# Attention feeding a gated feed-forward layer: visits of the attention stages one unit later, transposes of q behind the spread of the reciprocals, and finer dependencies of the output weights

## The chip, the core and the metric

The kernel runs on one core of one Trainium2 chip. The metric is the device time of one execution in microseconds (us); lower is better. Three runs of the kernel before gave a median of 535.46 us (535.23 to 538.49).

The core has a matrix engine (PE), a vector engine (DVE), an activation engine (ACT) and two engines that here do hardly more than start transfers: SP for stores, transposes and small copies, POOL for loads. Each engine works through its own instructions strictly in the order in which they stand in its program, and waits where one of them depends on something that isn't done.

## The reference

```python
def _attn_ref(q, k, v, E, F):            # q, k, v: 8 batches, 8 heads, 1024 x 64
    k_proj = np.einsum('ks,bhsd->bhkd', E, k)     # 1024 rows become 64
    v_proj = np.einsum('ks,bhsd->bhkd', F, v)
    scores = scale * np.matmul(q, k_proj.transpose(0, 1, 3, 2))
    ...
    attn = np.exp(scores)
    attn = attn / (np.sum(attn, axis=-1, keepdims=True) + 1e-09)
    return np.matmul(attn, v_proj)

def _moe_ref(x, w_gate, w_val, w_out):   # x: 8192 x 512, weights 512 x 1536 and 1536 x 512
    gate = 1.0 / (1.0 + np.exp(-(x @ w_gate)))
    val = x @ w_val
    return gate * val @ w_out
```

The attention's output, with its eight heads side by side, is `x` of the second function. All arrays are float32; the kernel computes in bfloat16 on PE with float32 sums.

## The kernel before, in words

**Blocks and units.** The 8192 rows are 16 blocks of 512, two for each batch. The feed-forward layer of a block is cut into three *units* K = 3 * block + (0, 1, 2); a batch b is units 6b to 6b+5, called u = 0 to 5. In one unit `g_chain` (L1746) computes a sixth of the gate and `v_chain` (L1775) a sixth of the value columns, each with seven half-size products of 4 matmuls (a Strassen-like scheme, so it needs sums of blocks of `x` and of weights beforehand: `xs_sums` L1589, `gt_sums` L1548, `vt_sums` L1519, all on DVE). Once a block's three units are done, `o_chain` (L1428) multiplies by the output weights `wO` with seven products in 14 groups of 6 matmuls, with the weight sums of `t_sums` (L1316): T2, T3 and T4 go to the tile `wT`, and T1 replaces the quarter B12 inside `wO`. Stores of the finished rows (`stored`, L1413) leave on SP.

**Attention.** While the feed-forward units of batch b run, the attention of batch b+1 is computed in short *visits* that borrow four of the eight PSUM banks (A0, F0, A3, F3, of which A0 and F0 are those of `g_chain`): `sc_visit` (L1170) computes the scores of four heads, and ACT takes their exponentials; there are two such visits. `den_visit` (L1186) follows the second: the denominators on PE, two reciprocals on DVE (`rec`, L959), and `spread` (L1126), which writes the reciprocals to DRAM (tile `rden` to `rd`, on SP) and, when that has landed, reads them back with eight broadcasting transfers of 256 KB (`xu<-rd` in the profile, L1146). `xo_visit` (L1178), twice, multiplies by v; `scaled` (L1155) on DVE multiplies the result with the spread reciprocals into `xT`, the input of the next batch's units. The first `xo_visit` needs the first four of the eight transfers. Then `kv` (L863) projects k and v of batch b+2 into 64 rows on PE; `keep_kd` (L879) copies the k part on ACT to `kpd`, and one transposing transfer on SP makes `kpD` of it, which the next `sc_visit` needs. `transpose_q` (L850) makes `qT` of the loaded `Qb` with four transposing transfers on SP. `load_q`, `load_k`, `load_v` (L423, L395, L405) bring 1 MB each from POOL. There is one `Qb`, one `qT`, one `kpD` and one pair of buffers for k and v.

**The places of the visits.** They are set in the loop over b, `late_` being 1 for b = 1 and 0 otherwise:

```python
            late_ = 1 if b == 1 else 0
...
                    if u == late_:
                        n["sc_visit"](t0 - 1.0, (0, 1), (GA, GC, XA, XB))
                    if u == late_ + 1:
                        n["sc_visit"](t0 - 1.0, (2, 3), (GA, GC, XA, XB))
                        n["den_visit"](t0 + 6.0, XA)
                        if b + 2 < B:
                            transpose_q()
```

So the visits of b = 1 lie in units 1, 2, 4, 5 (with `kv` in 5), and those of b = 2 to 6 in units 0, 1, 3, 4 (with `kv` in 4).

**What sets the order.** From unit 6 on, everything is noted as tasks, and `arranged` (L52) puts them in order: it goes through a model of the engines with fixed costs (`COST`, L28) and takes, whenever an engine is free, the ready task with the earliest due time. Due times come from the goals that are given to groups of matmuls (`PACE` is 9.9 us for a unit). The resulting order, not its times, becomes the program; `Plan.add` (L146) then finds what each instruction has to wait for, from the names that it reads (`r`) and writes (`w`). Units 0 to 5 are put in order by hand (`todo`, `put`, `on`, L1876 to L1977); their last steps are `kv2` (L1962), two of the weight sums (T4 and T1, `on(3, 4, ...)`, L1971) and the transposes of q (L1972). The first task of the planned part, `o_chain(1, ...)` (L1992), uses bank A2, which `kv2` used just before.

Of the kernel before, what the change touches and what calls it, by code (L numbers as in the profile page):

```python
# [7 lines left out]
ALU = mybir.AluOpType  # L8
# [22 lines left out]
class Task:  # L31
    def __init__(self, eng, call, t):
        self.eng, self.calls, self.goal = eng, [] if call is None else [call], None
        busy, tail = COST[eng]
        self.busy = busy if t is None else t
        self.lat = self.busy + tail
        self.dma = call is not None and call[5] is not None
        if self.dma:
            self.busy, self.lat = (0.85 if eng == "POOL" else 0.6), t if t is not None else 3.0
# [2 lines left out]
        return later.pre[self.n]  # L42

    def keys(self):
        r, w = set(), set()
        for c in self.calls:
            r.update(c[2])
            w.update(c[3] + c[4])
        return r - w, w, (r & w)
# [66 lines left out]
class Plan:  # L116
# [8 lines left out]
        self.tasks = None  # L125
        self.open = None

    def note(self, eng, call, t):
        if self.open is not None:
            assert eng == "PE"  # L130
            self.open.calls.append(call)
        else:
            self.tasks.append(Task(eng, call, t))

    @contextlib.contextmanager
    def group(self, goal, us):
# [6 lines left out]
        self.tasks.append(self.open)  # L143
        self.open = None

    def add(self, eng, fn, r=(), w=(), x=(), dma=None, t=None):  # L146
        if self.tasks is not None:
            self.note(eng, (eng, fn, tuple(r), tuple(w), tuple(x), dma), t)
            return None
        op = Op()  # L150
        op.eng, op.fn, op.dma, op.need = eng, fn, dma, False
        op.sem, op.val = None, 0
        deps = {}

        def dep(o, raw):
            if o is op:
                return
            if o.eng == eng and o.dma is None:
                if eng == "PE" or (eng != "POOL" and not raw):
                    return  # L160
            deps[id(o)] = o

        for k in r:
            for o in self.writers.get(k, ()):
                dep(o, True)
        for k in tuple(w) + tuple(x):
            for o in self.writers.get(k, ()):
                dep(o, False)
            for o in self.readers.get(k, ()):
                dep(o, False)  # L170
        for k in r:
            self.readers.setdefault(k, []).append(op)
        for k in tuple(w) + tuple(x):
            self.writers[k] = [op]
            self.readers[k] = []
        op.deps = list(deps.values())
        for o in op.deps:
            o.need = True
        if dma is not None:
            self.dma_count[dma] = self.dma_count.get(dma, 0) + 16  # L180
            op.sem, op.val = dma, self.dma_count[dma]
        self.ops.append(op)
        return op
# [46 lines left out]
def bass_linformer_attn__then__ffn_glu_sigmoid_kernel(  # L230
# [18 lines left out]
    with contextlib.ExitStack() as es:  # L249
# [6 lines left out]
        wT = sbuf("wT", [P, 3, NF // 2, 256], BF16)  # L256
# [54 lines left out]
        wO = sbuf("wO", [P, NF, DM], BF16)  # L311
        sigs = [sbuf(f"sig{i}", [P, 2, 512], FP32) for i in range(3)]
        sig = [sigs[i][:, 0, :] for i in range(3)]
        hT = [sbuf(f"hT{i}", [P, NF, 512], BF16) for i in range(2)]
# [17 lines left out]
        add = plan.add  # L332
# [514 lines left out]

            return qt, sc, den, bc, xo

        def transpose_q():  # L850
            for r in range(NR):
                add(
                    "SP",
                    lambda e, r=r: e.dma_start_transpose(
                        qT[:, 2 * r : 2 * r + 2, :].rearrange("p h (t c) -> p (h t) c", c=P),
                        Qb[:, 2 * r : 2 * r + 2, :].rearrange("p h c -> p (h c)"),
                    ),
                    r=[("Q", hf, r // 2) for hf in range(2)],
                    w=[("qT", r)] + [("qT", hf, r // 2, r % 2) for hf in range(2)],
                    dma=f"qT{r}",  # L860
                )

        def kv(b, bk):  # L863
# [413 lines left out]
        def oproj(blk, tt, pb, cols=((0, DM),)):  # L1277
            o = vsnap[tt][:, :] if tt < 2 else ost[:, tt, :]
            ok = [("vsnap", tt)] if tt < 2 else None
            t = 2 * (2 * (blk % 2) + tt % 2) + tt // 2  # L1280
            for n, (c0, c1) in enumerate(cols):
                if n:
                    pb = FF.take()
                for m in range(NF):
                    mm(
                        pb,
                        bank[pb][:, 0 : c1 - c0],
                        hT[blk % 2][:, m, tt * P : (tt + 1) * P],
                        wO[:, m, c0:c1],
                        [("hT", blk % 2, m, tt // 2), "wO"],  # L1290
                        start=(m == 0),
                        stop=(m == NF - 1),
                    )
                dve(
                    lambda e, pb=pb, c0=c0, c1=c1: e.tensor_scalar(
                        o[:, c0:c1], bank[pb][:, 0 : c1 - c0], 0.5, None, op0=ALU.mult
                    ),
                    [],
                    ok or [("ost", tt, x) for x in ((0, 1) if len(cols) == 1 else (n,))],
                    b=pb,  # L1300
                )
                FF.append(pb)
                add(
                    "SP",
                    lambda e, c0=c0, c1=c1: e.dma_start(out_v[blk // 2, t][:, c0:c1], o[:, c0:c1]),
                    r=ok or [("ost", tt, x) for x in ((0, 1) if len(cols) == 1 else (n,))],
                    dma=f"out{tt}" if n == 0 else "outlast",
                )
# [7 lines left out]
        def t_sums(n):  # L1316
            B11, B12 = wO[:, 0:H6, 0:256], wO[:, 0:H6, 256:512]
            B21, B22 = wO[:, H6:NF, 0:256], wO[:, H6:NF, 256:512]
            T4, T3, T2 = [wT[:, i, :, :] for i in range(3)]
            o, a, b, op, r, w = {  # L1320
                3: (T3, B22, B12, ALU.subtract, ["wO"], [("wT", 3)]),
                2: (T2, T3, B11, ALU.add, ["wO", ("wT", 3)], [("wT", 2)]),
                4: (T4, B21, T2, ALU.subtract, ["wO", ("wT", 2)], [("wT", 4)]),
                1: (B12, B12, B11, ALU.subtract, [], ["wO", ("wT", 1)]),
            }[n]
            if n == 4:
                w = w + ["bsel8", ("kp", 0), ("kp", 1)]
                w += [(k, R) for k in ("rhi", "rhl") for R in range(2)]
            dve(lambda e: e.tensor_tensor(o, a, b, op), r, w, t=0.95)
# [532 lines left out]
        def second_loads():  # L1862
            load_q(1)
            load_k(1)
            load_v(1)
            transpose_q()
            load(
                wO[:, :, :],
                moe_w_out.rearrange("(m p) c -> p m c", p=P),
                ["wO"],  # L1870
                "wO",
                r=turned()[:2],
            )
# [54 lines left out]
        def on(u, j, fn):  # L1928
            put(11 + 9 * u + j, fn)
# [38 lines left out]
            AA.append(bk)  # L1968

        on(3, 4, kv2)  # L1970
        on(3, 4, lambda: (t_sums(4), t_sums(1)))  # L1971
        on(3, 4, transpose_q)  # L1972
        for i, slot in enumerate(todo):
            slot()
# [14 lines left out]
        gt_sums(1)  # L1989
        for n in (1, 2, 3, 4):  # L1990
            xs_sums(2, n)
        o_chain(1, OA, OC, 0.0, 2.0, sums=False)  # L1992
        for n in (1, 2, 3, 4):
            xs_sums(3, n)
# [2 lines left out]
        for b in range(1, B):  # L1997
            n = attention(b + 1) if b + 1 < B else None
            if b + 2 < B:
                load_k(b + 2)  # L2000
                load_v(b + 2)
            late_ = 1 if b == 1 else 0
            for u in range(6):
                K = 6 * b + u
                t0 = when(K)
                if n is not None:
# [3 lines that stand above are left out]
                        n["sc_visit"](t0 - 1.0, (2, 3), (GA, GC, XA, XB))  # L2010
                        n["den_visit"](t0 + 6.0, XA)
                        if b + 2 < B:
                            transpose_q()
                        if b + 3 < B:
                            load_q(b + 3, n["spread_keys"])
                    if u == late_ + 3:
                        n["xo_visit"](t0 - 1.0, (0, 1), (GA, GC, XA, XB))
                    if u == late_ + 4:
                        n["xo_visit"](t0 - 1.0, (2, 3), (GA, GC, XA, XB))
                        for i in (1, 2, 3, 4):  # L2020
                            xs_sums(2 * b + 2, i)
                    if u == late_ + 4 and b + 2 < B:
                        with group(t0 + 5.0, 1.83):
                            kv(b + 2, XA)
                        keep_kd(XA)
                        vd_one(XA, 0)
                        vd_one(XA, 1)
# [46 lines left out]
```

## Time and profile before

| what | us |
|---|---|
| median of three runs | 535.46 (535.23 to 538.49) |
| the profiled execution: its whole time | 538.83 |
| its span, first to last instruction | 537.0 |
| PE busy in the span | 508.6 (95%) |
| DVE busy | 405.2 (75%) |
| ACT busy | 352.0 (66%) |
| mean granted clock of PE | 0.983 |

The profile is of one execution. A row of a timeline has the start in us, the duration, the engine (SPq is a transfer started by SP), the line of the kernel, the operation, the tiles as out<-in, the shapes, and how many instructions in a row were merged; in brackets stands how long the engine was idle before it, and what ended that. Nearly all matmuls have line L372, the helper `mm`, so one goes by tiles: `pA<-qT,kpD` are scores, `pA<-eT,dsel` denominators, `pA<-eT,vpD` the products with v, `pA<-KVs,EFT` is `kv`, and `pA<-xT,wG` the first product of a unit's `g_chain`. The trace also records when each transfer has landed.

PE works without a gap of more than 0.2 us in most of the span. By the waits, it is idle four times for longer than half a microsecond after 84 us.

### The profile page before, as it was taken

Reading aid. Unit: us, or ns where it says so; the run is one execution under the profiler, and the core shown is the slowest. Engines: PE = TensorE matmul, PEld = TensorE weight load, DVE = VectorE, ACT = ScalarE, POOL = GpSimd, SP = SyncE. Lnnn points to the kernel's source line nnn. Section 1 sums busy time; section 2 is a strip of 40 time slices with the busy share of each in tenths; the row PEclk is TensorE's granted clock in tenths of the full one; section 3 lists DMA queues with packets and bytes.
Section 4 is the critical chain, followed back from the end, with each engine's and each line's share of the span. In section 5 each row is a group of like instructions: output and inputs, shape, how many; then the busy total and the mean of one; then the engine's idle time right before and its main releaser. Section 6 shows DMA issues by size and latency. Waiting matters only on the chain.

```text
span 537.0 us, 11363 instructions
## 1 busy us (share of the span) xinstructions
PE 508.6 (95%) x4668; PEld 401.6 (75%) x4677; DVE 405.2 (75%) x670; ACT 352.0 (66%) x644; POOL 36.9 (7%) x52
## 2 busy tenths in 40 slices
PE   5999998996788999999999999999999999999996
PEld 4544544884666887888788887888788888888885
DVE  3648689674675879696978879696978879786874
ACT  2555663874365856887678856887678857676752
POOL 9310200100010001000010001000000000000000
PEclk9999998999698999999999999999999999999999
DMA  9999999898969297995969395966502090101113
GB/s 162 199 199 202 149 210 176 138 188 180 139 101 188 50 193 163 149 176 98 201 98 214 56 227 83 184 141 113 134 12 79 24 222 3 51 30 40 40 41 118
DMA packets 90692, 69.42 MB, mean 129 GB/s; under 512 B 35472, under 2 KB 82832, under 8 KB 90640
## 3 DMA queue, kind: packets, MB, share of 16 engines
q0 software_dynamic: 33984, 29.89, 36.8%
q1 hardware_dynamic: 56656, 38.81, 32.9%
q8 instruction: 36, 0.59, 0.5%
q14 instruction: 16, 0.13, 0.1%
HBM read 72.88 MB, written 17.56 MB: 168 GB/s over the span
## 4 chain that ended last, share of the span: by engine, by line
PE 88%; DMA 5%; DVE 3%; ACT 1%; issue 1%; POOL 1%; SPq 0%; DVEq 0%; ACTq 0%; POOLq 0%
PE pA L372 49%; PE pF L372 39%; DMA KVs<-in_v_dram 2%; DMA kpD<-kpd 2%; DMA xu<-rd 1%; DVE vsnap L1664 1%; DVE hT L1786 0%; DVE xT L800 0%; ACT kpd L376 0%; DVE hT L1264 0%; ACT vpD L376 0%; SPq L1146 0%; DVE hS L1345 0%; POOL KVs L390 0%; POOL Qb L390 0%
## 5 line engine op out<-in xcount | busy, mean ns | idle before, releaser
L376 ACT ACTIVATE sig<-pA 128x512 f32<-128x512 f32 x126 | 74.9, 595 | 51.2 <-PE pA L372 51.2
L1653 ACT ACTIVATE pF<-pA 128x512 f32<-128x512 f32 x99 | 58.0, 587 | 43.0 <-PE pA L372 29.9
L1664 DVE TENSOR_TENSOR vsnap<-pF,vsnap 128x512 f32<-128x512 f32 x90 | 62.0, 689 | 29.4 <-ACT vsnap L376 13.9
L1740 DVE TENSOR_TENSOR sig<-pF,sig 128x512 f32<-128x512 f32 x84 | 57.5, 684 | 23.1 <-PE pF L372 17.6
L372 PE MATMUL pF<-wO,hT 128*128 128x256 bf16 (+1 forms) x400 | 59.3, 286 | 0.2 <-issue 0.2
L1786 DVE SCALAR_TENSOR_TENSOR hT<-sig,vsnap 128x512 bf16<-128x512 f32 x84 | 57.2, 686 | 1.3
L376 ACT ACTIVATE sig<-sig 128x512 f32<-128x512 f32 x84 | 52.8, 630 | 7.8 <-DVE sig L1740 7.0
L372 PE MATMUL pF<-xS,wV 128*128 128x256 bf16 x360 | 55.0, 276 | 0.3
L376 ACT ACTIVATE vsnap<-pA 128x512 f32<-128x512 f32 x84 | 50.0, 595 | 7.4 <-PE pA L372 7.2
L372 PE MATMUL pA<-xT,vT 128*128 128x256 bf16 x336 | 51.0, 275 | 0.0
L372 PE MATMUL pF<-xT,wG 128*128 128x256 bf16 (+1 forms) x257 | 49.3, 312 | 1.5 <-DVE hT L1264 0.8
L372 PE MATMUL pA<-xT,gT 128*128 128x256 bf16 x336 | 50.5, 273 | 0.0
L372 PE MATMUL pF<-xS,wG 128*128 128x256 bf16 x336 | 50.4, 273 | 0.0
L376 ACT ACTIVATE sig<-pF 128x512 f32<-128x512 f32 x66 | 39.3, 596 | 14.9 <-PE pF L372 12.9
L372 PE MATMUL pA<-wT,hT 128*128 128x256 bf16 x360 | 48.8, 273 | 0.0
L372 PEld LDWEIGHTS pF<-wO,hT 128*128 128x128 bf16 x402 | 38.6, 98 | 10.9 <-issue 1.0
L372 PEld LDWEIGHTS pF<-xS,wV 128*128 128x128 bf16 x360 | 34.4, 99 | 10.7 <-issue 2.3
L372 PE MATMUL pF<-xT,wV 128*128 128x256 bf16 (+1 forms) x240 | 41.5, 294 | 0.0
L372 PEld LDWEIGHTS pA<-xT,vT 128*128 128x128 bf16 x336 | 31.6, 98 | 9.1 <-ACT sig L376 4.1
L372 PEld LDWEIGHTS pA<-wT,hT 128*128 128x128 bf16 x360 | 35.0, 98 | 4.6 <-issue 0.4
L1786 DVE SCALAR_TENSOR_TENSOR hT<-sig,pF 128x512 bf16<-128x512 f32 x42 | 28.6, 681 | 10.8 <-PE pF L372 10.6
L372 PEld LDWEIGHTS pF<-xS,wG 128*128 128x128 bf16 x336 | 32.9, 98 | 3.8
(150 smaller groups left out, 876.1 us busy)
## 6 DMA issues: line engine op xcount, KB each, us to landing
out_dram<-ost SPq DMA_DIRECT2D x61, 256.0 KB, 3.8
xu<-rd SPq DMA_DIRECT2D x48, 256.0 KB, 7.6
Qb<-in_q_dram POOLq DMA_DIRECT2D x7, 1024.0 KB, 9.3
KVs<-in_k_dram POOLq DMA_DIRECT2D x7, 1024.0 KB, 11.2
KVs<-in_v_dram POOLq DMA_DIRECT2D x7, 1024.0 KB, 16.0
wO<-in_moe_w_out_dram POOLq DMA_DIRECT2D x1, 1536.0 KB, 13.1
wG<-in_moe_w_gate_dram POOLq DMA_DIRECT2D x5, 256.0 KB, 18.2
wV<-in_moe_w_val_dram POOLq DMA_DIRECT2D x5, 256.0 KB, 18.8
```

Source lines behind the costliest of these rows:

```text
L372: return add("PE", lambda e: e.matmul(o, lhsT, rhs, **kw), r=r, x=[("bank", b)])
L376: return add("ACT", lambda e: e.activation(o, i, func, scale=scale), r=r, w=w, x=x, t=t)
L1653: lambda e: e.activation(bank[c][:, :], bank[a][:, :], AF.Copy, scale=1.0),
L1664: lambda e: e.tensor_tensor(o, bank[bk][:, :], o, ALU.add),
L1740: dve(lambda e: e.tensor_tensor(o, bank[bk][:, :], o, ALU.add), [key], [key], b=bk)
L1786: lambda e: e.scalar_tensor_tensor(o, sg.rearrange("p (j c) -> p j c", j=2), 1.0, x.rearrange("p (j c) -> p j c", j=2), ALU.add, ALU.mult,),
```

## The change

1. `late_` is 1 for every b. The visits of b = 2 to 6 lie in units 1, 2, 4, 5 like those of b = 1, one unit later than before, with everything that hangs on them: the reciprocals and their spread, the transposes and the load of q, `kv` with the transposing transfer of `kpD`, and the sums of `x` for the next batch's first block.
2. In the planned part `transpose_q` gets the names of the spread reciprocals as a *tie*. A tie counts as something read when `arranged` makes the order, and nowhere else: the four transposes are put behind the eight spread transfers in SP's order, but no wait is added to the program.
3. The weight sums T4 and T1 leave the handwritten part and become tasks of the planned part, behind the first sums of gate weights and of `x`.
4. The quarter B12 of `wO`, which T1 overwrites, gets a name of its own, `wO12`. T1 now reads `wO` and writes `wO12`; products that read other quarters no longer wait for it, and T3 and the undivided output product (L1289) read both names.

```diff
@@ class Task @@
+        self.tie = ()
...
     def keys(self):
-        r, w = set(), set()
+        r, w = set(self.tie), set()
@@ class Plan @@
-    def note(self, eng, call, t):
+    def note(self, eng, call, t, tie):
...
             self.tasks.append(Task(eng, call, t))
+            self.tasks[-1].tie = tie
...
-    def add(self, eng, fn, r=(), w=(), x=(), dma=None, t=None):
+    def add(self, eng, fn, r=(), w=(), x=(), dma=None, t=None, tie=()):
@@ transpose_q @@
-        def transpose_q():
+        def transpose_q(tie=()):
...
                     dma=f"qT{r}",
+                    tie=tie,
@@ oproj @@
-                        [("hT", blk % 2, m, tt // 2), "wO"],
+                        [("hT", blk % 2, m, tt // 2), "wO", "wO12"],
@@ t_sums @@
-                3: (T3, B22, B12, ALU.subtract, ["wO"], [("wT", 3)]),
+                3: (T3, B22, B12, ALU.subtract, ["wO", "wO12"], [("wT", 3)]),
...
-                1: (B12, B12, B11, ALU.subtract, [], ["wO", ("wT", 1)]),
+                1: (B12, B12, B11, ALU.subtract, ["wO"], ["wO12", ("wT", 1)]),
@@ second_loads @@
-                ["wO"],
+                ["wO", "wO12"],
@@ the handwritten part @@
-        on(3, 4, lambda: (t_sums(4), t_sums(1)))
         on(3, 4, transpose_q)
@@ the planned part @@
         for n in (1, 2, 3, 4):
             xs_sums(2, n)
+        t_sums(4)
+        t_sums(1)
         o_chain(1, OA, OC, 0.0, 2.0, sums=False)
...
-            late_ = 1 if b == 1 else 0
+            late_ = 1
...
                         if b + 2 < B:
-                            transpose_q()
+                            transpose_q(n["spread_keys"])
```

More of the change, by code (lines that the diff above doesn't have):

```diff
@@ L144, in group @@
         self.open = None
-    def add(self, eng, fn, r=(), w=(), x=(), dma=None, t=None):
+    def add(self, eng, fn, r=(), w=(), x=(), dma=None, t=None, tie=()):
         if self.tasks is not None:
-            self.note(eng, (eng, fn, tuple(r), tuple(w), tuple(x), dma), t)
+            self.note(eng, (eng, fn, tuple(r), tuple(w), tuple(x), dma), t, tie)
             return None
```

## The prediction

> **What bounds the kernel now.** The page comes first: PE is busy for 95% of the span, so only PE's idle time and what it does at half clock can be won without taking work away. Its row of granted clock has three dips.
>
> ```profile
> PE 508.6 (95%) x4668; PEld 401.6 (75%) x4677; DVE 405.2 (75%) x670; ACT 352.0 (66%) x644; POOL 36.9 (7%) x52
> PEclk9999998999698999999999999999999999999999
> ```
>
> Next the waits of PE after 84 us, which name the idle time; its three long pieces lie at the three dips.
>
> ```profile
> PE pA L372 <- DVE xT L1159: 8.3, 1, 8.3
> PE pA L372 <- DMA kpD<-kpd: 4.0, 1, 4.0
> PE pA L372 <- ACT vpD L376: 2.5, 1, 2.5
> PE pA L372 <- DVE hS L1345: 0.7, 1, 0.7
> ```
>
> Then the windows (length, busy us and instructions of each engine, granted clock, DMA): what follows the shortest of the three, the other two with what follows them, and the rest.
>
> ```profile
> 88.74:92.00 3.26, 3.26 (x17) 2.28 (x18) 3.26 (x7) 0.58 (x1) 0.00 (x0) 0.52 1.01 87
> 128.95:137.21 8.26, 0.00 (x1) 0.01 (x1) 0.75 (x2) 0.28 (x1) 0.00 (x0) 0.73 0.96 186
> 137.21:143.10 5.89, 5.89 (x28) 4.09 (x29) 3.53 (x6) 2.33 (x4) 0.43 (x1) 0.51 0.90 131
> 159.64:163.62 3.98, 0.00 (x0) 0.00 (x0) 0.23 (x1) 1.25 (x3) 0.00 (x0) 0.99 1.33 158
> 163.62:167.27 3.65, 3.65 (x22) 2.14 (x23) 0.72 (x2) 2.17 (x4) 0.00 (x0) 0.55 1.18 258
> 170.00:525.00 355.00, 354.73 (x3321) 297.86 (x3318) 290.19 (x456) 255.56 (x468) 7.87 (x9) 1.00 0.54 109
> ```
>
> After each wait PE runs at about half clock (0.52, 0.51, 0.55) for three to six us; from 170 to 525 us it is busy for 354.73 of 355 us. What is saved before 170 us therefore reaches the end, if the change opens no new gap later. Last, SP's timeline before the first wait:
>
> ```profile
> 120.58 1.23 SPq L854 DMA_TRANSPOSE qT<-Qb  x1
> 121.86 0.58 SPq L1129 DMA_DIRECT2D rd<-rden  x1
> 122.54 2.62 SPq L854 DMA_TRANSPOSE qT<-Qb  x2
> 125.20 1.07 SPq L1418 DMA_DIRECT2D out_dram<-ost  x2
> 126.32 6.07 SPq L1146 DMA_DIRECT2D xu<-rd  x8
> ```
>
> The reciprocals are done at 118.15 (DVE's row 116.38, 1.77 us). But SP's next instruction is a transpose that waits for q, landed at 120.57; `rd` leaves at 121.86 and lands at 123.90, and two more transposes and two stores stand ahead of the spread. Its fourth transfer, the last that the first `scaled` needs, lands at 136.24; DVE starts at 136.46, and PE, whose next product needs that bank, at 137.21.
>
> **The change, part by part.** A unit is one of the groups K; batch b is the round of the loop.
>
> *Transposes behind the spread, batch 1* (already at units 1, 2, 4, 5). `rd` can leave at 118.2. It lands after 2.0 us (this row) or 2.4 us (244.35 to 246.79, batch 3), here beside the end of the load of q; I take 120.6. The two stores are ready once DVE's row 119.21 (0.68) is over, so they take 119.9 to 121.0 by their 1.07 us, and the spread starts at 121.0. From its start to its fourth landing: 9.9 us here (126.32 to 136.24), 9.4 in batches 2 and 3 (246.81 to 256.21); behind stores, 9.9. So 130.9, plus the 0.97 us from landing to PE: 131.9. PE would wait 2.95 instead of 8.26 us: **5.3 saved**. Bounds: 0 (something else holds `rd`), and 8.26 (a spread that lands by 128.0).
>
> *The half clock behind it.* The 28 matmuls from 137.21 take 5.89 us; at 0.109 us each (the step in the full-clock rows) they take 3.06: 2.83 lost. After the wait of 3.99 us, 8 score matmuls (0.56 us in the row at 99.60) and 14 others (1.53) took 3.65: 1.56 lost. After the wait of 2.46 us, 16 took 3.24 instead of 1.75: 1.49 lost. For a wait of 2.95, between the last two, I take 1.5: **1.3 saved** (bounds 0 and 2.83).
> [...]
>
> *Scores of batch 2 one unit later.* Before, `kv` of batch 1 (151.72, unit 5) is followed by a visit in unit 0, and the transposing transfer lands at 163.58 where PE wants it at 159.64. The visit goes to unit 1, about ten us later. The wait of 3.99 goes, and its half clock, 1.56: **5.55 saved**. In later batches, where `kv` and scores are as far apart as they will be here, the visit starts 14.9 us after `kv` (211.23 to 226.09) and the transfer has landed 12.2 to 13.0 us after it (batch 4: 332.10, 345.14). Late next is that transfer, with about two us to spare.
>
> *Visits of batches 2 to 6 one unit later.* The same instructions in another place: 0 in PE work. What changes is what lies beside them.
> (a) Spread against the first `xo_visit`. In batch 3 the fourth transfer lands at 256.21, `scaled` starts at 256.43 and ends at 257.12, and PE's next `g_chain` starts at 257.73: so a landing until 256.8 (257.73 less 0.23 and 0.69) costs nothing: 0.6 us to spare, and the limit is 15.1 us after the denominators' start (241.66). In unit 2 the store pair that starts at 255.34, 27.8 us behind the batch's first product (227.53), comes at nearly the moment of `rd` (244.35 plus a unit of 10.1, 26.9 behind). Behind `rd`, it costs the spread 0.5 us (9.9 against 9.4); ahead of it, its 0.85 us of issue and the landing behind 512 KB (2.3 and 2.7 us for the pair of 125.20). Also one group of output products less falls between denominators and `xo_visit`, 0.66 us, since the goals of two chains leave a hole there. Against this stand batches 4 and 6, which land 1.5 and 2.0 us before they must. Bounds for a batch: 0 and 2 us of wait; nearest is batch 1's row, stores between `rd` and spread: 0.3. Five batches: **1.5 lost** (0 to 10, and half clock on top if waits reach 2.46 us). No gain is possible, as PE has no gaps there.
> (b) The four transposes (1.3 us of issue each; 2.8 and 4.3 us in batch 2, where two stand behind the spread) now always come behind it. Behind them wait on SP the next stores, due a half unit or more earlier or a unit later, and `kpD`, 20 us later. On POOL the load of q waits for the transposes: in batch 2 the last two land 16.3 us after the spread's start (186.65, 202.96); in batch 3 the load of q begins 15.4 after it (262.23). With all four behind the spread I estimate 19, or 24 after the denominators' start; the load takes 8.8 us (262.23) and ends at 33, where the loads of k and v begin (32.4: 241.66 to 274.09), beside which `kpD` travels. That can take its two us to spare, and is costed at 0 (0 to 1.5 for each of four batches).
> (c) `x` for the next batch is needed one unit sooner. Batch 1 shows that place: second `xo_visit` at 148.44, its sums done at 156.4, next first product at 159.6 or later had PE not waited. 0; without that cover, up to 3 us a batch.
>
> *T4 and T1 into the plan.* Two instructions of 0.95 us leave DVE's rows 86.53 and 87.39 and are placed later among its tasks. PE's start at 88.74 hangs on ACT's `vpD`, which ends at 88.60, so an earlier start of the weight sums gains 0; what hides the two later is DVE's idle time (1.67 us before 94.84 alone). Without it, 1.9 us.
>
> *The names wO and wO12.* T1 ended at 88.35, `vpD` at 88.60: the finer name lets PE start 0 us earlier.
>
> Sum: 5.3 + 1.3 + 5.55 − 1.5 = 10.65, a span of 526.35 instead of 537.0. The profiled execution took 538.83 in all, 3.4 more than the median of the runs, of which its span does not tell the cause; I take the saving from the median: 535.46 − 10.65 = 524.8, rounded to 525.
>
> **Rivals.**
> *All idle time returns.* If the spread lands by 128.0 and nothing is lost later: 8.26 + 2.83 + 5.55 = 16.6, **519**. For it: `rd` lands in 1.7 us elsewhere. Against it: 9.4 us of spread alone after 118.2 + 1.7 is 129.3.
> *The spread of batch 1 stays late.* Only the scores' wait goes: 535.46 − 5.55 = **530**. For it: the transfer of `rd` and the stores share the DMA with the load of q until 120.57, and stores started at 112.95 took 6.4 us beside it. Against it: the load is over when the spread starts.
> *Slower: the stores get ahead of `rd` in batches 2 to 6.* Product, copy and stores behind the denominators end some 4.0 us after these begin (0.55 + 0.66, ACT 1.75 as at 253.58 to 255.32, issue 1.07); `rd` lands 3 later, the spread's fourth 9.6 after that: 16.6 against a limit of 14.5 to 15.1. PE waits about 2 us and loses 1.5 at half clock, five times: 17.5 in place of the 1.5 above, so 535.46 − 12.15 + 17.5 = **541**. It decides from 2.4 us a batch, half clock included. For it: 0.6 us to spare in batch 3. Against it: the reciprocals are done 2.6 us after the denominators begin, before the stores can be ready (2.95 by these rows).
>
> **How the numbers follow.** Forecast (519.5 to 529 for itself) 0.62; all returns 0.12; spread stays late 0.12; slower case and its milder forms 0.14. The predicted time is the first, 525. The range of 519 to 533 leaves out the slower case, and takes in both rivals on the faster side and 8 us of (a) and (b). One per cent, about what a measurement of this kernel can tell from none, is 5.4 us: faster is below 530.1. The forecast and the first rival lie there, and a fourth of the second: 0.62 + 0.12 + 0.03 = 0.77. Within 1%: the rest of the second rival, 0.09, and a third of the slower case, 0.04: 0.13. Slower: 0.10.
>
> **What would show it.** Right: SP's rows in batch 1 read `rd`, stores, spread, transposes, with the spread from about 121; the wait for `xT` is near 3 us; none for `kpD`; in batches 2 to 6 no gap before `pA<-xT,wG` of over 1 us. Wrong: a wait for `xT` in every batch with stores ahead of `rd`; a wait for `kpD` beside a load of q; or a first wait that stays at 8 us.

## The result, and the profile after

The changed kernel is slower: 562.15 us median of four runs (558.66 to 567.05) against 536.31 for the kernel before in the same job. The ratio is 1.0455 [1.0388, 1.0521]; it leaves out the profiled run, which was disturbed and which the median holds. Forecast were 525 us, a range of 519 to 533, and faster. The profiled execution took 567.05 us with a span of 565.3, so 28.3 us more span are to be found (the medians differ by 25.8). Most lines of the helpers stand two or three further down in the changed kernel: L372 is L374, L376 is L378, L1146 is L1149, L1418 is L1421, L1653 is L1656.

Busy times and the granted clock from the page of the changed kernel:

```profile
PE 519.4 (92%) x4668; PEld 406.9 (72%) x4677; DVE 405.7 (72%) x670; ACT 349.0 (62%) x644; POOL 37.0 (7%) x52
PEclk9999998998999979999799998999889997999999
```

PE's work is the same 4668 matmuls, and the row of the clock has new dips, five groups of them, behind its first third. The waits of PE after 80 us say what stands there (engine, tile and line that wait, what they wait for: total, times, longest):

```profile
PE pA L374 <- ACT pF L1656: 26.4, 5, 6.1
PE pA L374 <- DVE xT L1162: 3.8, 2, 3.4
PE pA L374 <- ACT vpD L378: 2.4, 1, 2.4
PE pA L374 <- DVE hS L1348: 0.7, 1, 0.7
```

Two things are as forecast: the wait for `xT` is short, and `kpD` is gone from the list. On top stands a releaser that the list of before did not have at all, `pF` of L1656. It is a `seed`: ACT's copy of one bank into another, behind the first product of a chain and ahead of the second, which adds to the bank that was copied. The products that wait are `pA<-xS,gT`, the second of a `g_chain`, so these are seeds of `g_chain`. A seed has taken 0.6 us all along; now one comes late in each of batches 2 to 6. ACT's own list between 170 and 520 us says why:

```profile
ACT ost L378 <- DMA out_dram<-ost: 39.1, 5, 8.6
```

The instruction that ACT waits with is another one, `evac` of `o_chain`, which copies a finished product into the output rows `ost`; what it waits for is a store out of those rows. Here is the place in batch 2, the chain that ended last (start, us, what):

```profile
190.80 10.04 DMA out_dram<-ost
...
200.91 0.04 ACT ost L378
...
201.41 0.60 ACT pF L1656
...
202.06 1.04 PE pA L374 x4
```

A store that starts at 190.80 lands at 200.84. Nothing computes in between that this chain depends on. ACT's timeline of the same stretch has the wait in brackets, and PE's the wait for the `seed`:

```profile
192.58 0.58 ACT L378 ACTIVATE vsnap<-pA 128x512 f32<-128x512 f32 x1
200.91 0.60 ACT L378 ACTIVATE ost<-pF 128x512 f32<-128x512 f32 x1 [7.75 <-DMA out_dram<-ost]
201.41 0.59 ACT L1656 ACTIVATE pF<-pA 128x512 f32<-128x512 f32 x1
```

```profile
202.06 1.04 PE L374 MATMUL pA<-xS,gT 128*128 128x256 bf16 x4 [5.46 <-ACT pF L1656]
```

What the `seed` copies, the product `pA<-xT,wG` of 194.90, was done by 195.5; the `seed` still started only behind `evac`, at 201.41, 5.9 us later: ACT took the two in their order in its program. SP's timeline shows what the store stands behind:

```profile
181.81 0.81 SPq L1421 DMA_DIRECT2D out_dram<-ost  x2
182.66 0.45 SPq L1132 DMA_DIRECT2D rd<-rden  x1
184.90 5.21 SPq L1149 DMA_DIRECT2D xu<-rd  x8
190.16 1.08 SPq L1421 DMA_DIRECT2D out_dram<-ost  x2
191.34 12.02 SPq L856 DMA_TRANSPOSE qT<-Qb  x4
```

The pair of 190.16 leaves right behind the eight spread transfers, 2 MB in all. By the landing records the eighth of these lands at 198.38 and the pair at 200.11 and 200.84, ten us after issue. ACT was ready for `evac` at 193.16 (200.91 − 7.75), 3.0 us after the issue, and 3.0 us is what the planner's model gives a store (`t=3.0` in `stored`). The same batch before, SP and then ACT:

```profile
186.65 6.26 SPq L1146 DMA_DIRECT2D xu<-rd  x8
193.01 7.18 SPq L854 DMA_TRANSPOSE qT<-Qb  x2
200.29 2.09 SPq L1418 DMA_DIRECT2D out_dram<-ost  x4
```

```profile
207.06 0.60 ACT L376 ACTIVATE ost<-pF 128x512 f32<-128x512 f32 x1 [1.24 <-PE pA L372]
```

There the last of the spread landed at 200.38, just as the stores left; they took 3.2 to 3.6 us each, the last landed at 205.46, and `evac` waited for its product, not for them. Two windows of the changed kernel, PE's gap and what follows it (length, busy us and instructions of PE, weight loads, DVE, ACT, POOL, granted clock, DMA, GB/s) show what the wait costs:

```profile
196.59:202.06 5.47, 0.01 (x2) 0.01 (x1) 2.74 (x5) 1.15 (x3) 0.00 (x0) 0.92 1.24 205
202.06:208.00 5.94, 5.94 (x28) 4.20 (x29) 0.11 (x1) 2.83 (x5) 0.88 (x1) 0.50 0.56 92
```

5.46 us idle, then 28 matmuls at half clock. The five waits are 5.46, 5.16, 6.09, 4.34 and 5.38 us, 26.4 in all; half of PE's busy time inside the half-clock stretches behind them, 2.97, 2.75, 2.14, 2.45 and 2.47, is 12.8 more. Added over everything after 80 us until PE's last product, waits and half clock cost 49.58 us in the changed kernel (33.38 + 16.20) and 21.57 before (15.45 + 6.12): 28.0 of the 28.3 us.

The theory after this result, called A: the shift of the visits puts the store pair of rows 0 and 1 directly behind the spread; it lands late; the next block's `o_chain` rewrites just these rows first; its `evac` waits, ACT works in order, and the `seed` of a `g_chain` that stands behind it holds PE. Its rival, B: the transposes, now all behind the spread, delay what shares SP and the DMA with them.

### The profile page after: what moved, and what is told of

It is laid out like the page before. It is cut to its first block, busy times and chain, and to the rows that moved or that the text cites. A ratio compares the mean times of both kernels' runs of the same rounds, so it can differ in the third digit from the quotient of the medians.

```text
span 565.3 us, 11368 instructions
## 1 busy us (share of the span) xinstructions
PE 519.4 (92%) x4668; PEld 406.9 (72%) x4677; DVE 405.7 (72%) x670; ACT 349.0 (62%) x644; POOL 37.0 (7%) x52
## 4 chain that ended last, share of the span: by engine, by line
PE 78%; DMA 12%; DVE 5%; ACT 2%; issue 1%; POOL 1%; SPq 1%; ACTq 0%; DVEq 0%; POOLq 0%
PE pA L374 44%; PE pF L374 35%; DMA out_dram<-ost 8%; DMA KVs<-in_v_dram 2%; DMA xu<-rd 1%; DVE sig L1743 1%; DVE hT L1789 1%; DVE hS L1348 1%; DMA rd<-rden 1%; ACT pF L1656 1%; DVE hT L1348 0%; DVE xT L802 0%; DVE hT L1267 0%; ACT vpD L378 0%; SPq L1149 0%
## 5 line engine op out<-in xcount | busy, mean ns | idle before, releaser
L378 ACT ACTIVATE sig<-pA 128x512 f32<-128x512 f32 x126 | 74.9, 595 | 31.4 <-PE pA L374 31.4
L1656 ACT ACTIVATE pF<-pA 128x512 f32<-128x512 f32 x99 | 58.0, 587 | 47.0 <-PE pA L374 43.8
L378 ACT ACTIVATE vsnap<-pA 128x512 f32<-128x512 f32 x84 | 50.0, 596 | 18.8 <-PE pA L374 18.7
L374 PE MATMUL pF<-wO,hT 128*128 128x256 bf16 (+1 forms) x400 | 59.0, 285 | 0.2 <-issue 0.2
L378 ACT ACTIVATE sig<-sig 128x512 f32<-128x512 f32 x84 | 52.8, 628 | 8.0 <-DVE sig L1743 7.8
L374 PE MATMUL pF<-xS,wV 128*128 128x256 bf16 x360 | 54.2, 273 | 0.1
L374 PE MATMUL pF<-xT,wG 128*128 128x256 bf16 (+1 forms) x257 | 51.5, 323 | 1.5 <-DVE hT L1267 0.8
L374 PE MATMUL pA<-xT,gT 128*128 128x256 bf16 x336 | 52.8, 282 | 0.0
L374 PE MATMUL pA<-xS,gT 128*128 128x256 bf16 x168 | 27.8, 293 | 26.4 <-ACT pF L1656 26.4
L374 PE MATMUL pA<-wT,hT 128*128 128x256 bf16 x360 | 51.9, 284 | 0.0
L374 PE MATMUL pF<-xS,wG 128*128 128x256 bf16 x336 | 51.5, 277 | 0.0
L374 PE MATMUL pA<-xT,vT 128*128 128x256 bf16 x336 | 50.4, 273 | 0.0
L378 ACT ACTIVATE sig<-pF 128x512 f32<-128x512 f32 x66 | 39.4, 596 | 16.0 <-PE pF L374 13.9
L374 PEld LDWEIGHTS pF<-wO,hT 128*128 128x128 bf16 x402 | 37.9, 98 | 11.1 <-issue 1.0
L374 PEld LDWEIGHTS pF<-xS,wV 128*128 128x128 bf16 x360 | 33.7, 98 | 11.2 <-issue 5.1
L374 PE MATMUL pF<-xT,wV 128*128 128x256 bf16 (+1 forms) x240 | 41.5, 294 | 0.0
L374 PEld LDWEIGHTS pA<-wT,hT 128*128 128x128 bf16 x360 | 36.2, 102 | 6.7 <-issue 1.1
L374 PEld LDWEIGHTS pA<-xS,gT 128*128 128x128 bf16 x168 | 16.9, 103 | 30.3 <-ACT pF L1656 27.8
```

The lines of the kernel that those rows point to most:

```text
L374: return add("PE", lambda e: e.matmul(o, lhsT, rhs, **kw), r=r, x=[("bank", b)])
L378: return add("ACT", lambda e: e.activation(o, i, func, scale=scale), r=r, w=w, x=x, t=t)
L1656: lambda e: e.activation(bank[c][:, :], bank[a][:, :], AF.Copy, scale=1.0),
```

## The experiments

### Only the visits moved

Of the change, one line in the kernel before:

```diff
-            late_ = 1 if b == 1 else 0
+            late_ = 1
```

> The kernel before with the visits of batches 2 to 6 one unit later and nothing else. The transposes stand ahead of the spread again; the second store pair of a chain still stands right behind the eight spread transfers. Theory A (the copy into the output tile waits for that store pair, ACT stands still with it, and PE waits for the seed behind it): five waits of 4 to 6 us before the products of xS and gT as in the changed kernel, and the first wait of 8 us instead of 3.4: about 568 us. Theory B (the four transposes beside the stores hold them up): the five waits go, the score wait goes too: about 531.

567.85 us, ratio 1.0565 [1.0532, 1.0598]. Its waits of PE:

```profile
PE pA L372 <- ACT pF L1653: 24.8, 5, 5.5
PE pA L372 <- DVE xT L1159: 9.9, 2, 8.6
```

The whole loss is there without the transposes, and the long wait for `xT` of batch 1 with it; ACT waits 38.7 us for stores from `ost`. B falls as the cause of the loss.

### Only the transposes behind the spread

The tie of `transpose_q` alone, in the kernel before.

> The kernel before with the transposes behind the spread and nothing else; every engine but SP has the order of before. Both theories: the wait for xT in batch 1 falls from 8.3 to 3.4 us and its half clock from 2.8 to 1.5: 6 us less. The wait for kpD stays at 4. In batches 3 to 6 the second store pair now stands behind three transposes. Theory A: it lands at about 268 us in batch 3, where the next copy into the output tile starts at 267.5, so up to 1 us a batch is lost: 530 to 534. Theory B: the transposes ahead of it cost more, 2 to 4 us a batch: 535 to 545.

535.33 us, 0.9957 [0.9937, 0.9976]. Waits of PE after 80 us:

```profile
PE pA L374 <- DMA kpD<-kpd: 4.7, 1, 4.7
PE pA L374 <- DVE xT L1162: 3.6, 1, 3.6
...
PE pA L374 <- ACT pF L1656: 1.0, 1, 1.0
```

The wait for `xT` falls by 4.7 us, but part of that is spent again: the wait for `kpD` grows from 4.0 to 4.7 with 2.44 instead of 1.65 lost to half clock behind it, and in batch 3 a store pair behind three transposes (251.64, 8.11 us of issue) holds `evac` and the `seed` for 1.0 us. This part alone is worth 2.3 us, less than the 6.6 that the forecast gave it. The time lies just above the range set down for A (530 to 534) and at the edge of the one for B (535 to 545), so it does not part the two theories. The trace does: the transposes cost PE 1.0 us in one batch, not 2 to 4 in each. A delay of B's kind exists, and it is small.

### Only the sums and the finer name

T4 and T1 in the planned part, and `wO12`; the rest as before.

> The kernel before with T4 and T1 in the plan and the finer name, and nothing else. Both theories: 0, within 1 us of before (535 to 538), PE without new gaps.

536.32 us, 0.9974 [0.9956, 0.9993]: 1.3 us less, and 0.4 to 2.4 by the interval, where 0 was costed. PE has no new gap.

### The chain writes other rows first in every second block

In the changed kernel the two halves of `ost` change places for even blocks, so that a chain first rewrites the pair that was stored first, not the pair that was stored last. Place and order of all instructions stay; the late pair still lands late.

```diff
-        def quarter(tok, col):
+        def quarter(tok, col, blk=1):
+            tok ^= 1 - blk % 2
...
-                    lambda e, tt=tt, t=t: e.dma_start(out_v[blk // 2, t], ost[:, tt, :]),
-                    r=[("ost", tt, n) for n in range(2)],
+                    lambda e, row=row, t=t: e.dma_start(out_v[blk // 2, t], ost[:, row, :]),
+                    r=[("ost", row, n) for n in range(2)],
```

with `row = tt ^ (2 - 2 * (blk % 2))`, the name of the transfer by `row` too, and the block's number handed to `evac` and `add_snap`.

> The changed kernel, but chains of even blocks keep their first two rows of output tiles where odd blocks keep the last two. The copy that waited then writes a part of the tile whose stores left ten us earlier; the order of all five engines is that of the changed kernel, instruction for instruction, and the late store pair lands as late as there. Theory A: the five waits of 4.3 to 6.1 us and their half clock go: about 525, what was forecast for the change. Theory B, or any other that has ACT held by the transfers themselves: 555 or more.

526.44 us, 0.980 [0.9776, 0.9825]: faster than both kernels. SP and ACT of batch 2, then the first of PE's waits, which leaves `vpD` and `hS` as they were:

```profile
181.81 5.22 SPq L1149 DMA_DIRECT2D xu<-rd  x8
187.07 1.19 SPq L1423 DMA_DIRECT2D out_dram<-ost  x2
```

```profile
189.97 0.59 ACT L378 ACTIVATE ost<-pF 128x512 f32<-128x512 f32 x1
192.51 0.58 ACT L1658 ACTIVATE pF<-pA 128x512 f32<-128x512 f32 x1 [1.95 <-PE pA L374]
```

```profile
PE pA L374 <- DVE xT L1162: 4.5, 2, 2.8
```

The pair stands where it stood, behind the spread, and lands 8.3 and 9.1 us after its two issues at 187.07 and 187.71 (195.39, 196.78). But `evac` starts at 189.97 with no wait, and `pF` is gone from PE's list. All engines have the same instructions in the same order as in the changed kernel. So what costs is the reuse of the rows, not the late landing as such: A holds. The changed kernel itself has such a case: the pair at 289.19 and 289.59 took 9.0 and 10.0 us, beside the loads of k and v, and none of ACT's five long waits is for it.

### The planner is told what the store takes

The other way round: rows as in the changed kernel, and the true time in the model.

```diff
-                    t=3.0,
+                    t=(3.0 if tt > 1 else 10.0),
```

> The changed kernel, but the plan is told that the first store pair's rows (the pair that leaves last in a chain) take 10 us to land instead of 3. No name and no wait is changed, only the order that the plan makes: the pair now stands behind four spread transfers instead of eight, and the copy into the output tile stands behind the seed that PE needs, or some places further back, in ACT's order. Theory A (the plan's 3 us put the copy where ACT stands still with it): the 26 us of waits before xS and gT shrink to a few, 526 to 533. If they came from elsewhere than the copy's place: 555 or more.

528.18 us, 0.9845 [0.98, 0.989]. SP and ACT in batch 2:

```profile
182.59 2.58 SPq L1149 DMA_DIRECT2D xu<-rd  x4
185.21 1.07 SPq L1421 DMA_DIRECT2D out_dram<-ost  x2
186.33 3.31 SPq L1149 DMA_DIRECT2D xu<-rd  x4
```

```profile
193.29 0.58 ACT L1656 ACTIVATE pF<-pA 128x512 f32<-128x512 f32 x1 [2.44 <-PE pA L374]
...
196.72 0.60 ACT L378 ACTIVATE ost<-pF 128x512 f32<-128x512 f32 x1
```

With 10 us in the model the planner puts the pair behind four of the eight transfers, where it lands 6.5 and 6.2 us after issue (191.73, 192.06), and `evac` behind the `seed`. The five waits are gone. One number in the model was enough to undo the loss.

### Denominators two us earlier

The version with swapped rows, with `den_visit` at `t0 + 4.0` in place of `t0 + 6.0`.

> The changed kernel with swapped output rows, and the denominators' goal 2 us earlier. If the spread's fourth landing against PE's next product is what is left of the waits (2.84 us in batch 1, 1.70 in batch 5), these shrink to about 1 and 0: 523 to 525. If the denominators can't go earlier because the exponentials before them are late, or the stores now fall between reciprocals and spread: no gain, 526 to 528.

526.73 us, 0.9808 [0.9767, 0.985]: nothing beside the 526.44. The waits for `xT` (2.84, 1.65 and 0.35 us) add up to no less than with swapped rows alone (2.84 and 1.70). `rd` does leave two us earlier in batch 1 (115.15 against 117.12), but takes 4.67 us instead of 3.46 and lands only 0.8 us earlier. The hoped-for 523 to 525 was missed.

### The load of k behind `kpD`

The kernel before with the tie and the swapped rows, visits unmoved, and the load of k reading `kpD`, so that it starts behind it:

```diff
-                load_k(b + 2)
+                load_k(b + 2, [("kpD", 0)])
                 load_v(b + 2)
```

> The kernel before with the transposes behind the spread, swapped output rows, visits where they were before, and the loads of k and v made to wait for kpD. If the score wait came from kpD travelling beside those loads (8.8 us, against 2.7 in batch 5 where no loads run), kpD lands about 3 us after its start, and the wait of 4 to 4.7 us and its half clock go without any later visit: 526 to 529. If kpD is slow for another reason: 533 to 536.

531.6 us, 0.9897 [0.9856, 0.9937], but inconclusive for its question: the planner moved the load of v forward into the place that the load of k left, so `kpD` still travelled beside a load, 10.1 us (146.54 to 156.60), and PE waited 5.28 us for it. The time lies between the two outcomes expected.

### Both of these on the swapped rows

> The changed kernel with swapped output rows, the denominators' goal 2 us earlier, and the loads of k and v behind kpD. In the kernel with swapped rows alone PE no longer waits for kpD, so the later loads should add nothing to what the earlier denominators bring: 523 to 525, the same as that kernel within 1 us.

525.64 us, 0.9794 [0.9755, 0.9832]: the lowest median of all, just above the 523 to 525 expected, and within the intervals of the changed kernel with swapped rows and of that with earlier denominators. Neither addition shows.

### The load of q behind the spread

In batch 1 the transfer of `rd` took longer than in the later batches, and the load of q was my explanation. So, on the swapped rows, that load goes behind the spread of batch 1.

> The changed kernel with swapped output rows, and the load of q that ran beside the reciprocals of batch 1 put behind the spread. In that kernel rd took 3.5 us to land in batch 1 while q was still loading, 2.0 to 2.2 in later batches. If the load makes the difference, rd lands 2 us after its start; the two stores still stand ahead of the spread, so about 0.8 of the 2.84 us goes: 525 to 527. The transposes of that q come later in SP's order. If the load is not the reason, rd stays at 3.5 us.

527.69 us, 0.984 [0.9796, 0.9885]. `rd` leaves at 115.93. The DMA's busy tenths over 111 to 120 us, the instruction queue (q8) in them, and the transfer's time:

```profile
DMA  0999999200000000000000000293000006995699
...
q8 instruction: 1, 0.02, 1.1%
...
rd<-rden SPq DMA_DIRECT2D x1, 128.0 KB, 3.7
```

`rd` still takes 3.7 us, with nearly all DMA engines idle around it. The load of q is not the reason. The packets show what stands there instead: 120 of `rd`'s 128 packets of 1 KB start between 116.76 and 117.23 and the last eight, a sixteenth, only from 118.46 to 119.11; the one packet of the instruction queue, 16 KB, takes 1.60 us from 116.88. In the changed kernel it looks the same: the last eight start from 120.58 to 121.24, and such a packet takes 0.95 us from 119.65. The profiles before and after have 12 transfers of `rd` in batches 1 to 6. Two took 2.44 and 3.75 us (244.35 before, 118.02 after), and a 16 KB packet of the instruction queue runs during each of them; the other ten took 2.23 or less, and none has such a packet before its own last one has started. No run moved these packets, so this is a coincidence without exception in these two profiles and not a tested cause.

### Both loads behind `kpD`, visits unmoved

As the load of k above, and the load of v too.

> The kernel before with the transposes behind the spread, swapped output rows, visits where they were, and both loads, of k and of v, waiting for kpD (in the attempt before only that of k waited, and the plan put the load of v ahead of it). If kpD is slow because it travels beside those loads, it now lands 3 to 4 us after its start, PE's wait for it and its half clock go: 524 to 528. If not, kpD still takes 9 to 10 us and the wait of 5 us stays: 531 to 535.

526.08 us, 0.981 [0.9762, 0.9858]. The landing of `kpD` in batch 1, first with the tie alone, then here, and PE's longest wait here:

```profile
DMA to landing us min/median/max: 9.5/9.5/9.5
```

```profile
DMA to landing us min/median/max: 4.8/4.8/4.8
```

```profile
PE pA L374 <- DVE xT L1163: 3.4, 2, 3.1
```

The wait for `kpD` goes just as well by taking the loads of k and v out of its way as by asking for it a unit later. The gain does not need the move that cost so much.

### Swapped rows in the kernel before

A control: is the swap a gain by itself?

> The kernel before with swapped output rows and nothing else: a control. ACT doesn't wait for a store there, so nothing to win: 536 to 538, the waits of 8 and 4 us as before.

537.36 us, 1.0011 [0.9987, 1.0035]; the waits are 8.42 and 4.10 us as before. It is not: the swap only removes what the shift of the visits brings in.

## Why the prediction was wrong

**The step that failed** is "Visits of batches 2 to 6 one unit later", costed at 1.5 us (0 to 10); the runs show 39.2 us (26.4 of waits, 12.8 of half clock). The prediction looked at what the stores do to the spread: issue of 0.85 us ahead of it, 0.5 us behind `rd`. It did not look at what the spread does to the stores behind it. In its part (b) "the next stores, due a half unit or more earlier or a unit later" were cleared as neighbours of the transposes; in batch 2 the pair stood ahead of the transposes and directly behind the 2 MB. Nor did it ask who rewrites `ost`. That `evac` does, early in the next `o_chain`, was to be read in the kernel; that a `seed` of `g_chain` stands behind it on ACT is to be seen only in the order that the planner makes. What it did for the transposes, to name what waits behind them, it did not do for the spread, which had moved as well. A row that warned of it was in the prediction, "stores started at 112.95 took 6.4 us beside it", the load of q; it was used for batch 1 alone, and not to ask what a store costs in traffic elsewhere.

**The slower rival** had the sign and not the mechanism. The stores did get ahead of `rd` in batches 2 to 6 (181.81 and 182.66 in the changed kernel), as it says; yet `rd` landed 2.2 us after its issue (184.88) and `scaled` came in time, but for 0.47 us in one batch. In the version with swapped rows, where the order is the same, this costs 1.70 us once, not 17.5. What made the kernel slower was the other pair.

**What held.** Batch 1, SP in the changed kernel:

```profile
118.02 0.33 SPq L1132 DMA_DIRECT2D rd<-rden  x1
119.76 1.22 SPq L1421 DMA_DIRECT2D out_dram<-ost  x2
121.79 5.80 SPq L1149 DMA_DIRECT2D xu<-rd  x8
127.76 9.44 SPq L856 DMA_TRANSPOSE qT<-Qb  x3
```

The prediction had 118.2, 119.9, 121.0 and the fourth landing at 130.9; it was 131.18, and the wait for `xT` 3.36 us against 2.95. That the landing fits so well is in part luck, as two errors cancel: `rd` took 3.75 us instead of 2.0 to 2.4, so the spread began 0.8 us late, and its four transfers took 9.4 us instead of 9.9. Half clock behind the wait took 1.71 against 1.5. The wait for `kpD` and its half clock went, as the 5.55 us said: in the changed kernel it travels from 150.40 to 160.41 and nobody waits. T4, T1 and `wO12` were worth 1.3 us (0.4 to 2.4) against 0 costed.

**The sum without the failed step.** The terms that were meant to gain, 5.3 + 1.3 + 5.55, make 12.15. With swapped rows the kernel gains 11.2 us on its own before (537.64 − 526.44), though with another half-clock term than forecast: none is lost behind its 2.84 us wait, so 2.9 us are saved there and not 1.3. The other terms come out near their sizes in its profile: 5.4 for the wait for `xT` (5.3), 5.6 for `kpD` with its half clock (5.55), and 1.7 lost in batch 5 (1.5). The forecast of 525 was near the time that this change has once the rows are free; it missed the one wait that the change itself brings in.

## What to carry to other kernels

When transfers move, list for each queue what now stands behind them, and for each of those the next instruction that rewrites its source: here a late store cost nothing until an engine that works in order had to write those rows, and then it cost whatever stood behind that write on the engine. A planner's fixed time for a transfer fits some places and not others (3.0 us here, against 1.8 to 10.8 in the profile of the changed kernel); compare it with the landing behind the largest neighbour. A slower result can hide a good part: one part at a time, and then the wait alone taken away, showed a gain of 2% behind a loss of 4.5%.

## What the runs showed of the hardware

**In these runs half clock depended on where a gap lay, not only on its length.** The gap in which PE waits for `vpD` is 2.4 to 2.5 us long in all 13 profiles. Behind it the clock is at half before (0.52 from 88.74 to 92.00), in the changed kernel (0.50 from 88.53 to 91.94) and with swapped rows (0.72 from 86 to 92, gap included). It stays at full in five others: visits only, denominators earlier, both, late q and both loads, of which the last has 1.00 from 88 to 92. After 2.83 and 3.1 us (swapped rows, both loads) the clock stayed up; after 3.1 and 3.36 us (late q, changed) it fell. The traces before and after list the granted clock by time. Their half-clock stretches last 3.413, 6.827 or 10.240 us, but for the last, in which the program ends, and from the start of one to the start of the next it is 9, 13, 20, 27 or 109 times 3.413 us. Cut into steps of that length, the gaps of these two profiles sort themselves: from full clock it fell behind no step with up to 1.49 us of idle PE, and behind each of the twelve with 2.15 us or more; none lies between. Before, 2.15 of the first gap's 2.46 us lie in one step, and the clock falls; with only the visits moved, the gap is as long (2.5 us) and the clock stays up. Two windows show a longer gap, 2.83 us idle and what follows with swapped rows:

```profile
127.89:130.72 2.83, 0.00 (x0) 0.00 (x0) 0.74 (x2) 0.28 (x1) 0.00 (x0) 1.00 1.15 206
130.72:134.00 3.28, 3.27 (x30) 2.96 (x31) 3.28 (x6) 1.90 (x4) 0.00 (x0) 1.00 1.31 188
```

30 matmuls follow at full clock. The half clock behind the `vpD` gap of this profile starts between 88.2 and 89.0 (four matmuls from 88.20 take 0.77 us instead of 0.60, six from 88.76 take 1.49 instead of 0.82). Twelve steps later is 129.2 to 129.9, inside the gap, so by this estimate neither part of it is longer than about 2.0 us. So a forecast can't settle from its length whether a gap of 2.4 to 3.1 us, where these runs have both, is followed by half clock; it is a term of 0 or about 1.7 us, half of 3.413. The row that the prediction went by, half clock behind 2.46 us, was one of three such among these eight.

**In these runs a transfer's time depended on what was under way when it started.** A store of 256 KB took 2.1 to 2.7 us to land with little ahead of it (181.81 after, 125.20 before), 3.2 to 3.6 behind two transposes (200.29 before), 6.2 and 6.5 behind four spread transfers (batch 2 with the store time) and 7.8 to 10.0 behind eight (the five pairs of the changed kernel); beside the loads of k and v, on another queue, pairs took as long (9.0 and 10.0 us at 289.19). The issue of a transposing transfer took 1.23 and 1.29 us ahead of the spread (183.93 and 185.26 before); of the four behind the spread in batch 2 of the changed kernel the first two took 3.2 and 6.0 us and the last two 1.3. In batch 1 `kpD` took 8.8 to 10.1 us beside a load of k or v (before, changed, transposes only, late q) and 4.8 without them (both loads).
